# Loading half of the last piece of w_out earlier, swapping the engines that cast its rows, and moving one x step, in a fused attention and GELU kernel

## The chip, the cores and the metric

The kernel runs on one core of a Trainium2 chip. The metric is the device time of one execution in microseconds (us). A profiled execution also has a span, which is some 1.8 us shorter than its time.

## The reference

```python
def _attn_ref(q, k, v):              # 8 batches, 8 heads, 576 rows, 64 columns
    q_s = softmax(q, axis=-1)        # over the 64 columns   (written out in the original)
    k_s = softmax(k, axis=2)         # over the 576 rows
    kv = np.einsum('bhsd,bhse->bhde', k_s, v)
    return np.einsum('bhsd,bhde->bhse', q_s, kv)

x = attn_out.transpose(0, 2, 1, 3).reshape(4608, 512)
h = x @ w_in                         # 512 -> 2048
g = 0.5 * h * (1.0 + erf(h / sqrt(2)))
out = g @ w_out                      # 2048 -> 512
```

## The kernel before

A batch goes through these steps, and the words are used below as the program uses them. **exp_q, exp_k** (ScalarE), **norm_q** (VectorE and GpSimd: sums and a multiplication), **transposes** of q (TensorE) and their evacuation (the copy out of the memory that TensorE writes to) to qT, **kv** (TensorE, from exp(k) and the cast v), **x** = q times kv (TensorE), its evacuation to xT (ScalarE and VectorE), **h** = x times w_in (TensorE), **gelu** (ScalarE), **y** = g times w_out (TensorE), **y_out** (evacuation of y).

The y of batch 0 runs while batch 1's front is computed. Its w_out arrives in four pieces of four rows, where a row t is a set of 128 of its rows; a row t is cast to bf16 before the y matmuls of t. The change touches how the last piece (rows 12 to 15) comes in, and the order at the end of that stretch. All loads below are in one queue.

```python
    load_main(1, "q", q, 2)
    load_pair(1, "k", k, 2)             # batch 1's k in two halves
    wo.append(load_wo(3))               # rows 12 and 13 of w_out
    for hp in range(2):
        load_v1(hp)
    load_wo_row(wo[3], 2)               # row 14
    load_wo_row(wo[3], 3)               # row 15
    load_v1(2)
    load_v1(3)
    # ... cut ...
    exp_q(1, parts=2)
    exp_k(1, parts=2)
    table(AF.Gelu)
    cast_wo(2, wo[2])                   # rows 8 to 11, VectorE
    # ... cut: PSUM tiles ...
    norm_q(1, 0, 2)
    norm_q(1, 1, 2, nc.vector)
    cast_wo(3, wo[3], 0, 1)             # row 12, VectorE
    cast_wo(3, wo[3], 1, 1)             # row 13, VectorE
    for hp in range(HP):
        cast_v(1, hp, nc.gpsimd)
    # ... cut ...
    for t in range(12):
        y_part(t, range(J))             # four y matmuls a row
    load(3)
    cast_wo(3, wo[3], 2, 1, "s")        # row 14, ScalarE
    cast_wo(3, wo[3], 3, 1, "s")        # row 15, ScalarE
    y_part(12, range(J))
    y_part(13, range(J))
    tp_quarters(1, tps)                 # transposes
    kv_mm(1, 0)
    tp_quarters_evac(1, tps, 0, "v")
    tp_quarters_evac(1, tps, 1, "s")
    kv_norm(1, 0)
    y_part(14, range(J))
    y_part(15, (0, 1))
    # ... cut: tiles of x ...
    x_mm(1, 0)
    kv_mm(1, 1)
    y_out(0, yps[0], 0)
    x_evac(1, 0, "s")
    x_evac(1, 1)
    kv_norm(1, 1)
    y_out(0, yps[1], 1, "s")
    y_part(15, (2, 3))
    # then the h matmuls of batch 1
```

The softmax here doesn't subtract the row's maximum and nothing guards it: scores larger than these inputs give would overflow.

Of the kernel before, what the change touches and what calls it, by code (L numbers as in the profile page):

```python
# [8 lines left out]
FP32 = mybir.dt.float32  # L9
# [7 lines left out]
def kernel(  # L17
# [16 lines left out]
    nc = tc.nc  # L34
    B, H, S, D = q.shape
# [5 lines left out]
    HP = H // 2  # L41
    NDM = DM // 128
    NDF = DF // 128
    NS = S // 64
# [3 lines left out]
    f32in = ctx.enter_context(tc.tile_pool(name="f32in", bufs=2))  # L48
# [29 lines left out]
    def table(func):  # L78
        nc.scalar.activation(out=scr[:, 1:2], in_=scr[:, 0:1], func=func)  # L79

    st = [dict() for _ in range(B + 1)]

    def load_main(b, name, t, parts=1):
        f = f32in.tile([128, 2048], FP32, tag=name + "f")
        f = f.rearrange("p (h f) -> p h f", h=H)
        st[b][name + "f"] = f
        src = t[b, :, 0:M, :].rearrange("h (p j) d -> p h (j d)", j=J)
        n = H // parts
        for i in range(parts):
            nc.sync.dma_start(out=f[:, i * n:(i + 1) * n, :], in_=src[:, i * n:(i + 1) * n, :])  # L90

    def load_pair(b, name, t, parts=1):
        f = f32in.tile([128, HP, NS * D], FP32, tag=name + "f")
        st[b][name + "f"] = f
        src = t[b].rearrange("h (p n) d -> (h p) (n d)", n=NS).rearrange("(x q) f -> q x f", q=128)
        n = HP // parts
        for i in range(parts):
            h0 = i * n
            if b == 0 and name == "k" and i == 0:

                nc.scalar.dma_start(out=f[:, 0, :], in_=src[:, 0, :])
                h0 = 1
            nc.sync.dma_start(out=f[:, h0:(i + 1) * n, :], in_=src[:, h0:(i + 1) * n, :])

    def load_v1(i):

        if i == 0:
            st[1]["vf"] = f32in.tile([128, HP, NS * D], FP32, tag="vf", name="f")
        src = v[1].rearrange("h (p n) d -> (h p) (n d)", n=NS)
        nc.sync.dma_start(out=st[1]["vf"][:, i, :], in_=src[i * 128:(i + 1) * 128, :])  # L110

    def load(b):
        load_main(b, "q", q)
        load_pair(b, "k", k)
        load_pair(b, "v", v)
# [11 lines left out]
    def exp_q(b, parts=1):  # L127

        e = attn_sb.tile([128, J, H, D], BF16, tag="eq")
        st[b]["eq"] = e  # L130
        dst = e.rearrange("p j h d -> p h j d")
        src = st[b]["qf"]
        if b == B:
            src = src.rearrange("p j h d -> p h j d")
        else:
            src = src.rearrange("p h (j d) -> p h j d", j=J)
        if parts == 1:
            sets = [(slice(i, None, 4), slice(u, None, 4)) for i, u in ((0, 0), (1, 1), (2, 3), (3, 2))]
        else:
            sets = []  # L140
            for h in (0, 4):
                sets += [(slice(h + i, h + i + n), slice(h + u, h + u + n))
                         for i, u, n in ((0, 0, 2), (2, 3, 1), (3, 2, 1))]
        for i, u in sets:
            nc.scalar.activation(out=dst[:, i], in_=src[:, u], func=AF.Exp)  # L145

    def exp_k(b, parts=1):
        n = HP // parts
        for i in range(0, HP, n):
            nc.scalar.activation(  # L150
                out=ek[b % 2][:, i:i + n],
                in_=st[b]["kf"][:, i:i + n].rearrange("p x (n d) -> p x n d", n=NS),
                func=AF.Exp,
            )
# [33 lines left out]
    def kv_mm(b, half):  # L188


        if "kv" not in st[b]:
            kv_tiles(b)
        for n in range(NS):
            for i in range(2):
                for hh in range(2):
                    hp = 2 * half + i
                    pr = slice(hh * 64, hh * 64 + 64)
                    c = slice((hh ^ i) * 64, (hh ^ i) * 64 + 64)
                    nc.tensor.matmul(  # L199
                        st[b]["kv"][hp][c, 0:D + 1], ek[b % 2][pr, hp, n, :],  # L200
                        v_aug[b % 2][pr, hp, n, 0:D + 1], start=(n == 0), stop=(n == NS - 1),
                    )
# [25 lines left out]
    def norm_q(b, i=0, n=1, eng=None):  # L228

        eng = eng or nc.gpsimd  # L230
        eq = st[b]["eq"]
        w = H // n
        hs = slice(i * w, (i + 1) * w)
        qsum = small.tile([128, J, w], FP32, tag="qsum")
        recq = small.tile([128, J, w], FP32, tag="recq")
        nc.vector.reduce_sum(out=qsum, in_=eq[:, :, hs, :], axis=AX.X)  # L236
        nc.vector.reciprocal(recq, qsum)  # L237
        eng.tensor_tensor(  # L238
            out=eq[:, :, hs, :], in0=eq[:, :, hs, :],
            in1=recq.unsqueeze(3).to_broadcast([128, J, w, D]), op=ALU.mult,  # L240
        )
# [51 lines left out]
    def x_tile(b, hp, pool, tag):  # L293
        if "xT" not in st[b]:
            st[b]["xT"] = attn_sb.tile([128, HP, M], BF16, tag="xT", name="xT")
        st[b][f"x{hp}"] = pool.tile([128, M], FP32, tag=tag, name="ps")
# [32 lines left out]
    def x_evac(b, hp, eng="v"):  # L329
        ps = st[b][f"x{hp}"]  # L330
        if eng == "v":
            nc.vector.tensor_copy(out=st[b]["xT"][:, hp, :], in_=ps)  # L332
        else:
            nc.scalar.copy(out=st[b]["xT"][:, hp, :], in_=ps)  # L334
# [33 lines left out]
    def y_mm(c, ps, j, t):  # L368
        nc.tensor.matmul(  # L369
            ps, st[c]["g"][:, t, j * 128:(j + 1) * 128], wo_bf[:, t, :],  # L370
            start=(t == 0), stop=(t == NDF - 1),
        )

    def y_out(c, ps, j, eng="v"):
        y_sb = moe_sb.tile([128, DM], FP32, tag="y_sb")
        if eng == "v":
            nc.vector.tensor_copy(out=y_sb, in_=ps)  # L377
        else:
            nc.scalar.copy(out=y_sb, in_=ps)
        if c < B:  # L380
            dst = out[c * S:c * S + M, :].rearrange("(p j) n -> p j n", j=J)[:, j, :]
            nc.sync.dma_start(out=dst, in_=y_sb)
        else:
            for b2 in range(2):
                r0 = (2 * j + b2) * S + M
                nc.sync.dma_start(out=out[r0:r0 + R, :], in_=y_sb[b2 * R:(b2 + 1) * R, :])
# [69 lines left out]
    def load_wo(i):  # L456
        w = wst.tile([128, 4, DM], FP32, tag="w")
        src = moe_w_out[i * 512:(i + 1) * 512, :]
        if i == 0:
            for h in range(2):  # L460
                nc.sync.dma_start(
                    out=w[:, 2 * h:2 * h + 2],
                    in_=src[256 * h:256 * h + 256].rearrange("(p c) f -> p c f", c=2),
                )
            return w
        src = src.rearrange("(p c) f -> p c f", c=4)
        if i == 3:
            nc.sync.dma_start(out=w[:, 0:2], in_=src[:, 0:2])
            return w
        nc.sync.dma_start(out=w, in_=src)  # L470
        return w
# [5 lines left out]
    def cast_wo(i, w, c0=0, n=4, eng="v"):  # L477
        o, w = wo_bf[:, 4 * i + c0:4 * i + c0 + n, :], w[:, c0:c0 + n]
        if eng == "v":
            nc.vector.tensor_copy(out=o, in_=w)  # L480
        else:
            nc.scalar.copy(out=o, in_=w)
# [17 lines left out]
    wi = [load_wi(i) for i in range(5)]  # L500
    wo = [load_wo(i) for i in range(3)]
    load_main(1, "q", q, 2)
    load_pair(1, "k", k, 2)
    wo.append(load_wo(3))
    for hp in range(2):
        load_v1(hp)
    load_wo_row(wo[3], 2)
    load_wo_row(wo[3], 3)
    load_v1(2)
    load_v1(3)  # L510
    load(2)
    nc.vector.memset(zeros32, 0.0)  # L512
# [5 lines left out]
    table(AF.Exp)  # L518
    exp_q(0, parts=2)
    exp_k(0, parts=2)  # L520
    norm_q(0, 0, 2)
    norm_q(0, 1, 2, nc.vector)
# [48 lines left out]


    exp_q(1, parts=2)
    exp_k(1, parts=2)
    table(AF.Gelu)
    cast_wo(2, wo[2])
    tps = [pool.tile([128, HP, J, 64], BF16, tag=tag, name="tp")
           for pool, tag in ((psum_a, "a"), (psum_h, "h"))]
    yps = [psum_h.tile([128, DM], FP32, tag="h", name="ps") for j in range(2)]
    yps += [psum_y.tile([128, DM], FP32, tag="y", name="ps") for j in range(2)]  # L580
    norm_q(1, 0, 2)
    norm_q(1, 1, 2, nc.vector)
    cast_wo(3, wo[3], 0, 1)
    cast_wo(3, wo[3], 1, 1)
    for hp in range(HP):
        cast_v(1, hp, nc.gpsimd)

    def y_part(t, js):
        for j in js:
            y_mm(0, yps[j], j, t)  # L590
# [1 line left out]
    for t in range(12):  # L592
        y_part(t, range(J))
    load(3)
    cast_wo(3, wo[3], 2, 1, "s")
    cast_wo(3, wo[3], 3, 1, "s")
    y_part(12, range(J))
    y_part(13, range(J))
    tp_quarters(1, tps)
# [2 lines left out]
    tp_quarters_evac(1, tps, 1, "s")  # L602
    kv_norm(1, 0)
    y_part(14, range(J))
    y_part(15, (0, 1))
    x_tile(1, 0, psum_a, "a")
    x_tile(1, 1, psum_h, "h")
    x_mm(1, 0)
    kv_mm(1, 1)
    y_out(0, yps[0], 0)  # L610
    x_evac(1, 0, "s")
    x_evac(1, 1)
    kv_norm(1, 1)
    y_out(0, yps[1], 1, "s")
    y_part(15, (2, 3))



# [19 lines left out]

    exp_q(2, parts=2)
    exp_k(2)  # L640
    exp_k(3)
    exp_q(3)
# [73 lines left out]
```

## Time and profile before

| | before |
|---|---|
| time, median of the first 3 runs | 279.8 us (279.75 to 280.11) |
| span of the profiled run | 277.7 us |
| TensorE busy | 269.1 us, 97% of the span |
| first y matmul of batch 0 | 27.76 us |
| y matmul of row 12, due at 38.12 | 38.59 us |
| first h matmul of batch 1 | 43.92 us |

The last three rows are starts read from the timeline of TensorE. "Due" is the start that an unbroken stream would have had; the prediction works it out. A group in a timeline has its start, its length, the engine, the line, what is written and read, and the number of instructions; a bracket at the end names an idle time before the group and who ended it.

### The profile page before, as it was taken

How to read it: one execution, taken by the hardware profiler on the slowest of the kernel's cores; microseconds unless marked ns; L12 is line 12 of the kernel's file. 1: busy time of each engine (PE TensorE's matmuls, PEld its weight loads, DVE VectorE, ACT ScalarE, POOL GpSimd, SP SyncE). 2: the span in 40 equal slices, each digit the busy share in tenths (PEclk: the TensorE clock that was granted, in tenths of full speed). 3: DMA queues.
4: the chain of work that ended last, by engine and by line, in shares of the span. 5: the costliest groups of instructions: out<-in, count | busy, mean ns of one | idle time of the engine just before them, and what ended most of it. 6: DMA issues, size and time to landing. Idle time of an engine off the chain costs nothing.

```text
span 277.7 us, 4630 instructions
## 1 busy us (share of the span) xinstructions
PE 269.1 (97%) x1938; PEld 126.0 (45%) x1966; DVE 100.6 (36%) x154; ACT 158.9 (57%) x247; POOL 32.5 (12%) x26
## 2 busy tenths in 40 slices
PE   7899999999999999999999999999999999999995
PEld 3444444444444444444444444444444444444443
DVE  2876565319752540173008400751015200130012
ACT  4867586789377716791669246943683363126400
POOL 1510051002020220013000500050005000000000
PEclk9999999999999999999999999999999999999999
DMA  7999999964992149612980199117402500210033
GB/s 258 399 393 431 397 400 404 402 249 108 296 334 62 73 106 269 273 40 89 278 315 38 47 220 389 61 46 192 110 0 78 151 0 0 78 76 0 2 76 77
DMA packets 44980, 50.10 MB, mean 180 GB/s; under 512 B 20384, under 2 KB 29856, under 8 KB 44704
## 3 DMA queue, kind: packets, MB, share of 16 engines
q1 hardware_dynamic: 44560, 49.39, 52.8%
q10 hardware_dynamic: 400, 0.43, 0.5%
q8 instruction: 15, 0.25, 0.3%
q14 instruction: 5, 0.04, 0.1%
HBM read 36.70 MB, written 9.44 MB: 166 GB/s over the span
## 4 chain that ended last, share of the span: by engine, by line
PE 84%; DMA 11%; DVE 2%; issue 1%; ACT 0%; SPq 0%
PE ps L369 40%; PE ps L341 40%; DMA f<-in_q_dram 6%; DMA w<-in_moe_w_in_dram 3%; DMA f<-in_v_dram 2%; PE kv L199 2%; PE ps L308 1%; PE ps L394 1%; DVE qsum L236 1%; DVE e L238 1%; ACT e L145 0%; PE ps L313 0%; PE tp L272 0%; DVE recq L237 0%; DVE wo_bf L480 0%
## 5 line engine op out<-in xcount | busy, mean ns | idle before, releaser
L341 PE MATMUL ps<-xT,wi_bf 128*128 128x512 bf16 x557 | 124.1, 379 | 0.6
L369 PE MATMUL ps<-wo_bf,g 128*128 128x512 bf16 x543 | 122.1, 379 | 1.9 <-issue 1.1
L347 ACT ACTIVATE g<-ps 128x512 bf16<-128x512 f32 x142 | 83.5, 598 | 66.9 <-PE ps L341 66.8
L341 PEld LDWEIGHTS <-wi_bf 128*128 128x128 bf16 x576 | 56.4, 98 | 67.9 <-issue 0.5
L369 PEld LDWEIGHTS <-g 128*128 128x128 bf16 x560 | 54.0, 98 | 65.0 <-issue 1.0
L377 DVE COPY y_sb<-ps 128x512 f32<-128x512 f32 x33 | 22.7, 687 | 82.6 <-PE ps L369 79.5
L238 POOL TENSOR_TENSOR e<-e,recq 128x2048 bf16<-128x2048 bf16 (+1 forms) x9 | 25.7, 2855 | 176.6 <-DVE recq L237 148.5
L162 DVE CAST v_aug<-f 128x576 bf16<-128x576 f32 x24 | 16.4, 745 | 46.6 <-DMA f<-in_v_dram 46.6
L236 DVE TENSOR_REDUCE qsum<-e 128x16 f32<-128x1024 bf16 (+1 forms) x13 | 21.1, 1621 | 14.0 <-ACT e L145 14.0
L334 ACT CAST xT<-ps 128x512 bf16<-128x512 f32 x18 | 9.9, 588 | 26.8 <-PE ps L308 16.8
L145 ACT ACTIVATE e<-f 128x512 bf16<-128x512 f32 (+1 forms) x42 | 20.5, 556 | 3.7 <-DMA f<-in_q_dram 3.6
L150 ACT ACTIVATE ek<-f 128x2304 bf16<-128x2304 f32 (+1 forms) x10 | 17.2, 1728 | 0.5 <-DMA f<-in_k_dram 0.4
L332 DVE CAST xT<-ps 128x512 bf16<-128x512 f32 x17 | 11.0, 686 | 17.0 <-PE ps L308 14.1
L79 ACT ACT_TABLE_LOAD x9 | 11.5, 1283 | 2.8 <-issue 2.7
L487 PE MATMUL ps<-zeros 128*128 128x512 f32 x14 | 8.5, 772 | 1.5 <-DVE zeros L512 1.5
L145 ACT ACT_TABLE_LOAD x7 | 9.0, 1283 | 0.1
L446 DVE CAST wi_bf<-w 128x512 bf16<-128x512 f32 x12 | 7.1, 621 | 2.3 <-DMA w<-in_moe_w_in_dram 1.9
L199 PEld LDWEIGHTS <-ek 64*64 64x64 bf16 x576 | 6.4, 105 | 2.1 <-issue 0.5
L199 PE MATMUL kv<-v_aug,ek 64*64 64x65 bf16 x576 | 6.8, 193 | 0.4 <-POOL v_aug L162 0.4
L238 DVE TENSOR_TENSOR e<-e,recq 128x1024 bf16<-128x1024 bf16 x4 | 6.3, 1574 | 0.1
L487 PEld LDWEIGHTS ps<-zeros 128*128 128x128 f32 x14 | 3.4, 252 | 5.7 <-issue 4.3
L308 PE MATMUL ps<-qT,kvc 64*64 64x512 bf16 x62 | 5.6, 390 | 0.3 <-DVE kvc L218 0.2
(40 smaller groups left out, 49.5 us busy)
## 6 DMA issues: line engine op xcount, KB each, us to landing
out_dram<-y_sb SPq DMA_DIRECT2D x32, 256.0 KB, 2.4
f<-in_k_dram SPq DMA_DIRECT2D x6, 1152.0 KB, 9.8
f<-in_v_dram SPq DMA_DIRECT2D x6, 1152.0 KB, 11.6
f<-in_q_dram SPq DMA_DIRECT2D x6, 1024.0 KB, 7.7
w<-in_moe_w_in_dram SPq DMA_DIRECT2D x6, 512.0 KB, 9.0
f<-in_v_dram SPq DMA_DIRECT2D x8, 288.0 KB, 6.3
f<-in_q_dram SPq DMA_DIRECT2D x4, 512.0 KB, 8.8
w<-in_moe_w_out_dram SPq DMA_DIRECT2D x2, 1024.0 KB, 11.8
```

Source lines behind the costliest of these rows:

```text
L79: nc.scalar.activation(out=scr[:, 1:2], in_=scr[:, 0:1], func=func)
L145: nc.scalar.activation(out=dst[:, i], in_=src[:, u], func=AF.Exp)
L150: nc.scalar.activation(out=ek[b % 2][:, i:i + n], in_=st[b]["kf"][:, i:i + n].rearrange("p x (n d) -> p x n d", n=NS), func=AF.Exp,)
L162: eng.tensor_copy(out=o, in_=i)
L199: nc.tensor.matmul(st[b]["kv"][hp][c, 0:D + 1], ek[b % 2][pr, hp, n, :], v_aug[b % 2][pr, hp, n, 0:D + 1], start=(n == 0), stop=(n == NS - 1),
L236: nc.vector.reduce_sum(out=qsum, in_=eq[:, :, hs, :], axis=AX.X)
L238: eng.tensor_tensor(out=eq[:, :, hs, :], in0=eq[:, :, hs, :], in1=recq.unsqueeze(3).to_broadcast([128, J, w, D]), op=ALU.mult,)
L341: nc.tensor.matmul(ps, wi_bf[:, dm, t * 128:(t + 1) * 128], st[c]["xT"][:, dm, :], start=(dm == 0), stop=(dm == NDM - 1),)
L347: nc.scalar.activation(out=st[c]["g"][:, t, :], in_=ps, func=AF.Gelu)
L369: nc.tensor.matmul(ps, st[c]["g"][:, t, j * 128:(j + 1) * 128], wo_bf[:, t, :], start=(t == 0), stop=(t == NDF - 1),)
L377: nc.vector.tensor_copy(out=y_sb, in_=ps)
L487: nc.tensor.matmul(ps, z[:, 0:128], z, start=True, stop=True)
```

## The change

The intent is to take the hole at row 12 out of TensorE's stream. The first half of the last w_out piece goes ahead of the second half of batch 1's k; ScalarE casts rows 12 and 13 between the two halves of exp(k), and VectorE takes rows 14 and 15. Since the stream then runs earlier, the first x is put one y matmul later, so that the kv step behind it does not meet a v that is still being cast, and two y_outs go ahead of x.

```diff
@@ loads @@
     load_main(1, "q", q, 2)
-    load_pair(1, "k", k, 2)
+    load_k1(0)
     wo.append(load_wo(3))
+    load_k1(1)
@@ batch 1's front @@
     exp_q(1, parts=2)
-    exp_k(1, parts=2)
+    exp_k(1, parts=2, part=0)
+    cast_wo(3, wo[3], 0, 1, "s")
+    cast_wo(3, wo[3], 1, 1, "s")
+    exp_k(1, parts=2, part=1)
     table(AF.Gelu)
...
     norm_q(1, 1, 2, nc.vector)
-    cast_wo(3, wo[3], 0, 1)
-    cast_wo(3, wo[3], 1, 1)
...
-    cast_wo(3, wo[3], 2, 1, "s")
-    cast_wo(3, wo[3], 3, 1, "s")
+    cast_wo(3, wo[3], 2, 1)
+    cast_wo(3, wo[3], 3, 1)
@@ end of batch 0's y @@
     y_part(14, range(J))
-    y_part(15, (0, 1))
+    y_part(15, (0, 1, 2))
+    y_out(0, yps[0], 0)
+    y_out(0, yps[1], 1, "s")
     # tiles of x
     x_mm(1, 0)
     kv_mm(1, 1)
-    y_out(0, yps[0], 0)
     x_evac(1, 0, "s")
     x_evac(1, 1)
     kv_norm(1, 1)
-    y_out(0, yps[1], 1, "s")
-    y_part(15, (2, 3))
+    y_part(15, (3,))
```

(`load_k1` loads one half of batch 1's k; `exp_k` gets an argument for one half.)

More of the change, by code (lines that the diff above doesn't have):

```diff
@@ L103, in load_pair, with load_k1 @@
             nc.sync.dma_start(out=f[:, h0:(i + 1) * n, :], in_=src[:, h0:(i + 1) * n, :])
+    def load_k1(i):
+        if i == 0:
+            st[1]["kf"] = f32in.tile([128, HP, NS * D], FP32, tag="kf", name="f")
+        src = k[1].rearrange("h (p n) d -> (h p) (n d)", n=NS).rearrange("(x q) f -> q x f", q=128)
+        nc.sync.dma_start(out=st[1]["kf"][:, 2 * i:2 * i + 2, :], in_=src[:, 2 * i:2 * i + 2, :])
     def load_v1(i):
@@ L145, in exp_q, with exp_k @@
             nc.scalar.activation(out=dst[:, i], in_=src[:, u], func=AF.Exp)
-    def exp_k(b, parts=1):
+    def exp_k(b, parts=1, part=None):
         n = HP // parts
-        for i in range(0, HP, n):
+        for i in range(0, HP, n) if part is None else (part * n,):
             nc.scalar.activation(
```

## The prediction

> **What bounds the kernel now.** I read the page's busy line and its chain that ended last first, then the list of waits, then the timeline of the stretch that the change touches (36 to 46 us), engine by engine.
>
> ```profile
> PE 269.1 (97%) x1938; PEld 126.0 (45%) x1966; DVE 100.6 (36%) x154; ACT 158.9 (57%) x247; POOL 32.5 (12%) x26
> ...
> PE 84%; DMA 11%; DVE 2%; issue 1%; ACT 0%; SPq 0%
> ```
>
> TensorE has work in 97% of the span, and 84% of the chain that ended last is TensorE; the rest is the front (loads and batch 1's softmax) that a step of TensorE once waited for. So a change can only pay by closing a hole in TensorE's stream. The chain shows one such hole after the start, at the row of w_out that the change is about:
>
> ```profile
> 33.56 1.23 DVE qsum L236
> 34.79 0.02 issue
> 34.82 0.25 DVE recq L237
> 35.07 1.12 DVE qsum L236
> 36.19 0.02 issue
> 36.22 0.26 DVE recq L237
> 36.48 0.02 issue
> 36.50 1.70 DVE e L238
> 38.20 0.35 DVE wo_bf L480
> 38.55 0.04 issue
> 38.59 1.89 PE ps L369 x8
> ```
>
> The columns are start, duration and what (us). VectorE normalises batch 1's q until 38.20, only then casts row 12 of w_out, and the y matmuls of that row start at 38.59. The timeline of TensorE around it:
>
> ```profile
> 27.76 10.52 PE L369 MATMUL ps<-wo_bf,g 128*128 128x512 bf16 x47
> 38.59 1.89 PE L369 MATMUL ps<-wo_bf,g 128*128 128x512 bf16 x8 [0.30 <-DVE wo_bf L480]
> 40.40 0.71 PE L272 MATMUL tp<-identity,e 64*64 64x64 bf16 x64
> 40.93 0.54 PE L199 MATMUL kv<-v_aug,ek 64*64 64x65 bf16 x36
> 41.40 1.47 PE L369 MATMUL ps<-wo_bf,g 128*128 128x512 bf16 x5
> 42.80 0.41 PE L308 MATMUL ps<-qT,kvc 64*64 64x512 bf16 x4
> 43.04 0.51 PE L199 MATMUL kv<-v_aug,ek 64*64 64x65 bf16 x36
> 43.48 0.60 PE L369 MATMUL ps<-wo_bf,g 128*128 128x512 bf16 x2
> ```
>
> The printed wait is 0.30, counted from the end of a matmul that is still draining. The loss is larger. Twelve rows times four matmuls at one every 0.216 us from 27.76 put the next start at 27.76 + 48 x 0.2159 = 38.12; it came at 38.59. **The hole costs 0.47 us.** Nothing else there is a wait: the steps from transposes to kv, to y, to x leave 0.09 to 0.14 us each, as the same steps do in later batches where all operands are old (there they are the 0.05 and 0.16 us "issue" pieces). From 46 us on, the list of waits has no TensorE wait of note, so what TensorE gains or loses before 46 us should be carried to the end unchanged.
>
> **What the Trainium skill says.** (1) "TensorE: Matmul & The Clock Gate", section "Wait — 56ns, not 53.3ns?": warm matmuls of 512 columns start 215.7 ns apart. The trace agrees: 22 y matmuls in 4.91 us, the last one 0.38 long, make (4.91 - 0.38) / 21 = 0.216 us. (2) "DMA: Bandwidth & Descriptors", section "Queues, rings and completion order": each DMA engine takes descriptors in ring order. Here batch 1's two k halves and the first half of the last w_out piece were issued in that order and landed in it, about 35.1, 36.5 and 37.75; so issuing the w_out half before the second k half should swap the two landings. (3) "ScalarE: Activation LUTs", section "What ACT_TABLE_LOAD costs": 1283 ns for the load and about 1380 ns of drain for a switch of set. The trace has the 1.28 us, but the next activation begins right behind (37.72 + 1.28, then 39.01), so I charge 1.28 alone. (4) "Perfetto Trace Analysis", section "Optimizing Scalar/DVE Operations", says that breaking up instructions may let work complete sooner where these engines are not saturated but cause bubbles elsewhere. That is the case; the row casts were already split, and the change moves two of them to the engine that is free earlier.
>
> **The change part by part.** Nothing is added or removed but one split of an existing pair of issues: same bytes, same four row casts, same matmuls; two casts trade VectorE for ScalarE and the other two the reverse.
>
> Rows 12 and 13. The landing views and ScalarE's timeline give the times:
>
> ```profile
> DMA to landing us min/median/max: 9.0/9.0/9.0
> ...
> 35.11 1.16 ACT L150 ACTIVATE ek<-f 128x1152 bf16<-128x1152 f32 x1 [0.19 <-DMA f<-in_k_dram]
> 36.54 1.16 ACT L150 ACTIVATE ek<-f 128x1152 bf16<-128x1152 f32 x1 [0.26 <-DMA f<-in_k_dram]
> 37.72 1.28 ACT L79 ACT_TABLE_LOAD   x1
> 39.90 1.25 ACT L482 CAST wo_bf<-w 128x512 bf16<-128x512 f32 x2 [0.69 <-DMA w<-in_moe_w_out_dram]
> ...
> 41.30 1.37 POOL L162 CAST v_aug<-f 128x576 bf16<-128x576 f32 x2 [1.30 <-DMA f<-in_v_dram]
> ```
>
> The w_out half was issued at 28.75 and landed 9.0 later, 37.75. Put ahead of the second k half it lands 512 KB after the first: the stretches view gives 404 GB/s between 12 and 50 us, so 1.30 us after about 35.1, at 36.4. ScalarE has finished the first half of exp(k) at 35.11 + 1.16 = 36.27, so it casts from 36.4: row 12 at 36.4 + 0.62 = 37.0, row 13 at 37.65 (0.62 a row, from the 1.25 for two). TensorE wants row 12 at 38.12 and row 13 at 38.98. Both are over a microsecond early. **Gain: the whole 0.47 us**, at that place.
>
> Second half of exp(k). It lands at 37.75 instead of 36.5, runs to 38.9, the table load goes to 40.2, its dummy activation to 40.4. ScalarE then evacuates the transposes, which TensorE, now 0.47 earlier (39.93 to 40.46), hands over at about 40.7 (before: 0.8 after their start). No wait on the path.
>
> Rows 14 and 15 on VectorE. Row 14 lands at 39.90 and takes 0.41 there (the two casts before took 0.41 each), 40.31; TensorE wants it after the first kv half, at 41.40 - 0.47 = 40.93. Row 15 lands about 256 KB later, 40.5, cast by 40.95, wanted at 41.8. The VectorE evacuation of transposes then starts at 40.95 rather than 40.7, ends 41.65, kv norm 42.1.
>
> First x one group later. x now follows seven y matmuls: 40.93 + 7 x 0.216 + 0.1 = 42.54, against 42.80. Its operands are there at 42.1. kv of the second half follows at 42.78; its last v cast on GpSimd ends at 41.30 + 1.37 = 42.67. Just free: in the old order x would start at 42.33 and kv would have waited, which is what this part of the change is for.
>
> What it costs. Behind that kv half only one y matmul is left in place of two, so the h matmuls that need x follow sooner. Before, x at 42.80 was followed by ScalarE's evacuation from 43.25 to 43.84 and the h matmul at 43.92, with no gap. Now: x 42.54, evacuation 42.99 to 43.58 (0.45 after x and 0.59 long, as before; y_out of yps[1] on ScalarE is ahead of it, from about 42.46 to 43.05, just about fitting), so x is usable at 43.65. TensorE is through with kv and the one y matmul at 42.54 + 0.68 + 0.23 = 43.45. **New wait: about 0.20 us.** The second x half, its kv norm and the two remaining y_outs end well before they are wanted.
>
> Sum: -0.47 + 0.20 = -0.27 us; 279.8 - 0.27 = 279.5.
>
> **The rivals.** (a) The hole goes and no wait replaces it: -0.47, 279.3. For it: the 0.20 rests on delays of 0.45 and 0.07 us taken from single instructions. Against: the y matmul was the only cover. (b) The wait is moved, not removed: if landings come in order but later, or if ScalarE's later exp(k) and table load push the evacuation of transposes beyond 41.0, x waits for it, and with GpSimd's v casts, which are tied to the landings and not to TensorE, nothing of the gain is left: 279.8. GpSimd's slack is only about 0.1 us, so this is the serious one. (c) The reorder disturbs the queue, for example the blocked issue at 23.5 us (5.1 us long for one k half) now holds others up, and batch 1's front slips by some tenths: 280.1. Against it: the DMA share is full throughout and bytes are unchanged. (d) Front jitter: the hole hangs on the q load that ends near 32.3; in executions where it lands later the hole is wider than 0.47, and the change, whose rows have 1.1 us of slack, gains more: down to 279.2.
>
> **Range and chances.** The largest part possible is half a microsecond in 280, or 0.2%; the three runs before spread over 0.36 us. No rival reaches 2% (5.6 us) in either direction. I take 279.5, with (a) and (d) at the low end and (b) and some of (c) at the high one: 279.1 to 279.9. Faster by over 2%: 0.005; within 2%: 0.99; slower: 0.005.
>
> **What would show it.** Right: no TensorE wait on wo_bf near 38.1; the y stream of 27.8 us runs on for 56 matmuls, transposes near 39.9; ScalarE casts two rows between the halves of exp(k) near 36.4; x near 42.5; a wait of TensorE on xT of 0.1 to 0.3 us near 43.5; the gelu stream from 46 us on some 0.27 us earlier, and the end too. Step wrong: row casts on ScalarE after 38 (the landing did not move), a wait of the second kv half on v_aug (rival b), an x that waits for qT. The total would be wrong if any load that is first used after 46 us arrived later, or if the front (q's first half, 32.3 us) moved.

## The result, and the profile after

The changed kernel took 279.31 us in the median of 6 runs (279.26 to 279.55); the kernel before, with three more runs, 279.73 (279.33 to 280.11). The ratio is 0.9988, with a 95% interval of 0.9975 to 1.0001. Ratios are the mean time of one kernel's fast runs over that of the other's of the same rounds, so not quite the ratio of the medians.

From the page of the changed kernel, the busy line and the chain that ended last:

```profile
PE 270.9 (98%) x1966; PEld 125.6 (45%) x1966; DVE 100.8 (36%) x154; ACT 158.9 (57%) x247; POOL 32.5 (12%) x26
...
PE 94%; DMA 4%; POOL 0%; DVE 0%; issue 0%; SPq 0%
```

The busy sums of TensorE are not to be compared: the first trace has 1938 of its matmul records, this one 1966. The chain can be: 94% of it is TensorE now, and the 11% that went through loads in the kernel before is 4%, because no step in the middle of the stream waits for batch 1's softmax any more. Now the timeline of TensorE in the changed kernel, the same stretch as in the prediction:

```profile
27.79 12.25 PE L376 MATMUL ps<-wo_bf,g 128*128 128x512 bf16 x56
39.97 0.71 PE L279 MATMUL tp<-identity,e 64*64 64x64 bf16 x64
40.50 0.54 PE L206 MATMUL kv<-v_aug,ek 64*64 64x65 bf16 x36
40.97 1.68 PE L376 MATMUL ps<-wo_bf,g 128*128 128x512 bf16 x7
42.58 0.41 PE L315 MATMUL ps<-qT,kvc 64*64 64x512 bf16 x4
42.82 0.51 PE L206 MATMUL kv<-v_aug,ek 64*64 64x65 bf16 x36
43.26 0.39 PE L376 MATMUL ps<-wo_bf,g 128*128 128x512 bf16 x1
43.67 1.02 PE L348 MATMUL ps<-xT,wi_bf 128*128 128x512 bf16 x4
```

All 56 y matmuls run in one piece: the hole is gone. The x step starts at 42.58 where it started at 42.80. And the last y matmul, at 43.26, is followed by the first h matmul 0.41 us later; two matmuls of 512 columns start 0.216 to 0.23 apart, so this is a new gap of 0.18 us. It carries no bracket because the modelled end of the y matmul hides it. ScalarE in the same trace shows both the new casts and the cause of the gap:

```profile
34.91 1.16 ACT L157 ACTIVATE ek<-f 128x1152 bf16<-128x1152 f32 x1 [0.19 <-DMA f<-in_k_dram]
36.13 1.14 ACT L489 CAST wo_bf<-w 128x512 bf16<-128x512 f32 x2
37.56 1.16 ACT L157 ACTIVATE ek<-f 128x1152 bf16<-128x1152 f32 x1 [0.29 <-DMA f<-in_k_dram]
...
42.47 0.59 ACT L386 COPY y_sb<-ps 128x512 f32<-128x512 f32 x1 [0.69 <-PE ps L376]
43.04 0.59 ACT L341 CAST xT<-ps 128x512 bf16<-128x512 f32 x1
```

Rows 12 and 13 are cast right behind the first half of exp(k), 1.4 us or more before TensorE wants them. The evacuation of x ends at 43.04 + 0.59 = 43.63, and the h matmul that reads it starts at 43.67.

The first h matmul of batch 1 comes at 43.67 against 43.92, 0.25 us earlier, and the shift stays: the second kv step of later batches starts at 64.71 against 64.97 and the one of batch 7 at 184.71 against 184.97. From the first h matmul of batch 1 to the last matmul of the kernel the two traces have 230.19 and 230.20 us.

This gives a measure that is far finer than the times. **Start of h** is the start of the first h matmul of batch 1 less that of the first y matmul, both read from the timeline: 43.92 - 27.76 = 16.16 before, 43.67 - 27.79 = 15.88 after. In all fourteen traces what follows it takes 230.19 to 230.20 us, so a difference in it is a difference in the time, apart from where the stream begins. That start is not fixed either: the first y matmul comes at 27.76 to 28.32 us in these traces, and this enters the time in full.

### The profile page after: what moved, and what is told of

Same layout as the page of the kernel before. It is cut to its first block, busy times and chain, and to the rows that moved or that the text cites. A ratio compares the mean times of both kernels' runs of the same rounds, so it can differ in the third digit from the quotient of the medians.

```text
span 277.5 us, 4658 instructions
## 1 busy us (share of the span) xinstructions
PE 270.9 (98%) x1966; PEld 125.6 (45%) x1966; DVE 100.8 (36%) x154; ACT 158.9 (57%) x247; POOL 32.5 (12%) x26
## 4 chain that ended last, share of the span: by engine, by line
PE 94%; DMA 4%; POOL 0%; DVE 0%; issue 0%; SPq 0%
PE ps L348 44%; PE ps L376 44%; DMA f<-in_v_dram 2%; PE kv L206 2%; PE ps L315 2%; DMA f<-in_q_dram 2%; PE ps L401 1%; PE pair L348 1%; POOL v_aug L169 0%; PE ps L320 0%; PE tp L279 0%; SPq L103 0%; DVE kvc L225 0%; DVE y_sb L406 0%; DVE rec L224 0%
## 5 line engine op out<-in xcount | busy, mean ns | idle before, releaser
L376 PE MATMUL ps<-wo_bf,g 128*128 128x512 bf16 x560 | 124.1, 379 | 0.0
L487 DVE CAST wo_bf<-w 128x2048 bf16<-128x2048 f32 (+1 forms) x5 | 4.5, 907 | 6.1 <-DMA w<-in_moe_w_out_dram 6.1
```

The costliest lines, as they stand in the source:

```text
L376: nc.tensor.matmul(ps, st[c]["g"][:, t, j * 128:(j + 1) * 128], wo_bf[:, t, :], start=(t == 0), stop=(t == NDF - 1),)
```

## The experiments

Three quantities of each trace are used: the start of h as above; the **hole** before row 12, that is the start of the transposes less that of the first y matmul less the 12.18 us of an unbroken stream; and the **phase** p, the start of the first half of batch 1's exp(k) on ScalarE (which waits for its load) less that of the first y matmul. The phase tells how late the loads of q and k are against TensorE; it changes when the loads land earlier or later, and also when TensorE's y stream itself begins earlier or later. All three are worked out from the starts before rounding.

| trace | p | hole | start of h |
|---|---|---|---|
| before | 7.35 | 0.47 | 16.16 |
| before again | 7.33 | 0.45 | 16.14 |
| x later only | 7.00 | 0.11 | 15.99 |
| load order only | 6.92 | 0.04 | 15.73 |
| before, delayed | 7.76 | 1.04 | 16.74 |
| change | 7.12 | 0 | 15.88 |
| change again | 6.88 | 0 | 15.88 |
| change, delayed | 8.13 | 0 | 16.37 |
| y_out behind | 7.55 | 0 | 15.88 |
| no cover | 7.07 | 0 | 16.10 |
| casts, old loads | 7.05 | 0.02 | 15.90 |
| casts only | 7.45 | 0 | 16.07 |
| kv pair by pair | 6.83 | 0 | 15.83 |
| split cast | 6.82 | 0 | 15.70 |

**The change again.** No edit.

> The changed kernel unaltered, with five rounds, to narrow the ratio (0.9988 so far, its interval reaching 1.0001). My theory, from the two traces (hole of 0.47 us gone, a new wait of about 0.18 us on xT, all later starts 0.25 us earlier up to the last matmul): ratio 0.9991, 0.25 us faster. Rival (front jitter: executions of the kernel before in which batch 1's q lands later lose more than 0.47): ratio 0.9985 to 0.9988, and a spread of the kernel before of 0.5 us or more against about 0.3 for this one. In its trace: y stream of 56 matmuls without a break, first h matmul of batch 1 about 0.41 us after the last y matmul before it instead of 0.22.

It took 279.42 us (279.34 to 279.67), the kernel before in the same rounds 279.68 (279.26 to 279.84): ratio 0.9996 (0.9983 to 1.0008). So the gain is in neither call clear of zero, and it was smaller here. The trace has the same start of h to the hundredth, 15.88, with the loads 0.24 us earlier against TensorE (p 6.88 instead of 7.12): within this range the changed kernel does not depend on them. The kernel before spread more in these rounds too, 0.58 against 0.33 us, but over nine runs against five (more on this below).

**Casts only, x in its old place.**

```diff
-    y_part(15, (0, 1, 2))
-    y_out(0, yps[0], 0)
-    y_out(0, yps[1], 1, "s")
+    y_part(15, (0, 1))
     ...  (the tail of the kernel before)
```

> The new load order and row casts, but x and its y_outs in their old place (x after six y matmuls, two y matmuls left behind kv). My theory: x starts near 42.37, the second kv half begins near 42.6 but must wait for GpSimd's last v cast (ends about 42.77) at its first use of the fourth pair, so it ends about where it ends in the changed kernel; the two y matmuls behind it then cover x's evacuation, no wait on xT; first h matmul at about 43.70, within 0.05 us of the changed kernel's 43.67. So moving x is worth nothing: 0.22 to 0.25 us faster than before, equal to the change. Rival (the move is needed: the wait on v_aug comes on top): first h matmul at 43.9 or later, gain 0.05 us or less.

It took 279.33 us (279.19 to 279.54), ratio 0.9989 (0.9976 to 1.0003), which can't be told from the change. In its trace the wait on v is there as forecast:

```profile
42.42 0.41 PE L315 MATMUL ps<-qT,kvc 64*64 64x512 bf16 x4
42.66 0.20 PE L206 MATMUL kv<-v_aug,ek 64*64 64x65 bf16 x2
43.07 0.47 PE L206 MATMUL kv<-v_aug,ek 64*64 64x65 bf16 x34 [0.21 <-POOL v_aug L169]
```

Two kv matmuls run, then the third stops for the last v cast. The loads of this execution came late (p 7.45), so the stop was 0.39 us (from the due start 42.67 to 43.07) and the start of h 16.07, not the 15.85 or so that I had expected. So my theory that moving x is worth nothing failed in this trace, and the rival's number was met: the first h matmul came at 43.92, as in the first trace of the kernel before. The times, 0.9989 here against 0.9996 for the change in the same rounds, do not show that loss. What follows from the trace is that the move of x trades this wait, which varies with the loads, for the fixed one on xT.

**x later only.** The kernel before with the tail of the change.

```diff
-    y_part(15, (0, 1))
+    y_part(15, (0, 1, 2))
+    y_out(0, yps[0], 0)
+    y_out(0, yps[1], 1, "s")
     ...  (the tail of the change)
```

> The kernel before with only x one matmul group later and its y_outs ahead. My theory: the hole of 0.47 us at the row of w_out stays, the new wait on xT of about 0.2 us comes on top: 0.2 us slower than before (ratio 1.0007), first h matmul near 44.1 against 43.92. Rival (the move is harmless by itself and the missing gain is elsewhere): equal to before, no wait at the first h matmul.

Ratio 1.001 (0.9998 to 1.0023), median 279.76 us: slower by about what was expected, though the interval touches one. The trace is clear: start of h 15.99 = 15.69 + 0.11 of hole + 0.19 of the new gap. The surprise is the hole of 0.11, where the same code in the first trace of before had 0.47. Everything up to row 12 is equal in the two programs; what differs is that the loads stood 0.35 us earlier against TensorE (exp(k) began 0.13 us earlier, and the y stream 0.22 us later). This changed my theory: **the hole is not a constant of the program.** With VectorE's chain from the landing of q to the cast of row 12 being fixed in length, the hole should be p - 6.88, and zero below.

**kv pair by pair.** The casts-only kernel; in the second kv half of batch 1 the loop over pairs of heads is outermost, so that the last v is wanted later.

```diff
-        for n in range(NS):
-            for i in range(2):
+        order = [(n, i) for n in range(NS) for i in range(2)]
+        if (b, half) == (1, 1):
+            order = [(n, i) for i in range(2) for n in range(NS)]
+        for n, i in order:
```

> As the casts-only kernel, but the second kv half of batch 1 does all nine steps of its first pair of heads before those of its second pair, so that the last v cast on GpSimd is wanted some 0.2 us later. My theory: neither the wait on v_aug nor the one on xT is left; x near 42.37, first h matmul near 43.50, 0.17 us earlier than in the changed kernel, and 0.4 us faster than before (ratio 0.9985). Rival ([...]the kv half takes up to twice its 0.41 us): first h matmul at 43.7 or later and no gain over the change.

Start of h 15.83: no wait on v nor on xT, but the kv half, which is followed by y 0.44 us after its start otherwise, took 0.58 (42.79 to 43.37). So 0.05 us was gained over the change instead of 0.17, and the rival's size was largely right. The absence of the wait on v is no merit of the new order, though: in this execution the last v cast ended at 42.54, before the kv half began at 42.79, so that the old order would not have waited either. Ratio 0.9995 (0.9983 to 1.0008).

**Before again, and the useless load.** The next three runs test the dependence on the loads. The first has no edit. The other two are the kernel before and the change with 256 KB more in the queue ahead of batch 1's q:

```diff
+    nc.sync.dma_start(out=zeros32, in_=moe_w_out[0:128, :])
     load_main(1, "q", q, 2)
```

(The tile's memset and the warm-up are moved ahead of the loads in the program text; their order on the engines is unchanged.)

> The kernel before, unaltered: the noise of a ratio of equals, and a further trace of the hole. The traces so far say that the hole is set by how late batch 1's loads land against TensorE's stream: take p, the start of the first half of exp(k) of batch 1 less the start of the first y matmul. With p = 7.35 (first trace of before) the hole was 0.47, with p = 7.00 (x later only, same front) 0.12. My theory now: hole = p - 6.88, zero below, so here anything from 0 to 0.6 us, and that formula within 0.05. Rival: the hole is a fixed 0.47 us of the program, whatever p. Ratio 1.0000 with an interval of about 0.0012 to either side.

> The kernel before with one useless load of 256 KB put into the queue ahead of batch 1's q (into the tile of zeros that the warm-up matmuls have done with), so that all of batch 1's loads land about 0.65 us later against TensorE. My theory: p becomes 7.5 to 8.1, the hole p - 6.88, so 0.6 to 1.2 us, and the time 0.4 to 0.65 us longer than before (ratio 1.0015 to 1.0023). Rival (front not bound by these landings): no change.

> The changed kernel with the same useless load. My theory: rows 12 and 13 still come in time, so no hole at the row of w_out, but the last v cast gates the second kv half: excess over a stream without waits is the larger of 0.19 and p - 7.2, so 0.3 to 0.9 us; the change stays ahead of the delayed kernel before by about 0.3 us and by no more, since the next load of the same queue gates behind the one that was moved. Rival (the change takes the stream off the landings altogether): excess stays near 0.19, the time equals that of the undelayed change, and the lead over the delayed kernel before grows to 0.6 us or more.

Before again: ratio 0.9998 (0.9986 to 1.001), so two equal kernels differ by up to that interval; its hole is 0.45 with p 7.33, as p - 6.88 says, but a hole fixed at 0.47 would look the same there; what speaks against that rival is the delayed run and the two small holes. Its five runs spread over 0.18 us only, while eleven runs of the same kernel in the same rounds spread over 0.78. Before, delayed: 280.13 us, ratio 1.0031 (1.0018 to 1.0044), above the forecast of 1.0015 to 1.0023, though the interval reaches into it; in the traces its start of h is 0.58 us later than in the first of before. The hole shows in its timeline:

```profile
27.81 10.52 PE L369 MATMUL ps<-wo_bf,g 128*128 128x512 bf16 x48
39.21 1.89 PE L369 MATMUL ps<-wo_bf,g 128*128 128x512 bf16 x8 [0.88 <-DVE wo_bf L480]
```

Due at 27.81 + 10.36 = 38.17, the row came at 39.21: 1.04. The formula gives 0.88 for p 7.76, so it is 0.16 off here. Some 0.06 of it is that the two halves of q's exponentials ran without the pause that the other four traces with a hole on VectorE's path show, and p is measured behind them. The rest is VectorE's chain: from its first qsum to the cast of row 12 it took 4.65 us (34.08 to 38.73) against 4.56 (33.56 to 38.12), so the chain is not quite fixed in length. Change, delayed: 279.88 us, ratio 1.0013 (1.0001 to 1.0025). Its stream still has all 56 y matmuls in one piece, and waits further on:

```profile
40.54 0.78 PE L206 MATMUL kv<-v_aug,ek 64*64 64x65 bf16 x36
...
43.15 0.20 PE L206 MATMUL kv<-v_aug,ek 64*64 64x65 bf16 x2
43.57 0.47 PE L206 MATMUL kv<-v_aug,ek 64*64 64x65 bf16 x34 [0.23 <-POOL v_aug L169]
43.98 0.39 PE L376 MATMUL ps<-wo_bf,g 128*128 128x512 bf16 x1
44.20 1.03 PE L348 MATMUL ps<-xT,wi_bf 128*128 128x512 bf16 x4
```

The second kv half stops for the last v, and behind it y and h follow without the gap, since xT is ready by then. The first kv half stops too: after two matmuls it waits for the second v cast, which ends at 40.78, and y follows 0.71 us after its start instead of 0.47. Together with 0.05 before x these two stops, 0.24 and 0.39, make the 0.68 us by which the start of h exceeds 15.69. The expected p - 7.2 would be 0.93: p does not fix when the last v is cast, which ended 7.56 us after the start of exp(k) here and 7.86 us after it in the trace of the change. So the change does not take the stream off the loads: it moves the place where they bind from row 12 to the casts of v. The lead over the delayed kernel before is 0.0018 of the time, 0.5 us, between the 0.3 that I expected and the 0.6 of the rival; in the two traces it is 16.74 - 16.37 = 0.37, though the loads stood 0.37 us later in the second. The start of h of the delayed change is 0.49 us later than that of the undelayed one, so the rival's claim that it would not notice the delay falls.

**Split cast.** The casts-only kernel with the last v cast shared by GpSimd and ScalarE.

```diff
-    for hp in range(HP):
+    for hp in range(HP - 1):
         cast_v(1, hp, nc.gpsimd)
+    cast_v_part(1, 3, 0, 5, nc.gpsimd)
...
     tp_quarters_evac(1, tps, 1, "s")
+    cast_v_part(1, 3, 5, 9, nc.scalar)
```

> The casts-only kernel (x in its old place) with the last v cast of batch 1 split: its first five of nine steps on GpSimd, the other four on ScalarE, which is idle there. My theory: the last operand of the second kv half is ready some 0.3 us earlier, so neither v_aug nor xT is waited for unless p is above 7.3; first h matmul 15.69 to 15.75 us after the first y matmul, against 15.88 in both traces of the change, and about 0.19 us faster than the change in the mean (ratio to before about 0.9983 to 0.999). Rival (the wait on v_aug is one for the landing, not for the cast): first h matmul at 15.85 or later.

Start of h 15.70, the stream without any wait (15.69), and 0.18 us less than the change:

```profile
42.77 0.51 PE L214 MATMUL kv<-v_aug,ek 64*64 64x65 bf16 x36
43.21 0.61 PE L384 MATMUL ps<-wo_bf,g 128*128 128x512 bf16 x2
43.65 1.03 PE L356 MATMUL ps<-xT,wi_bf 128*128 128x512 bf16 x4
```

The times can't show it: 279.31 us, ratio 0.9996 (0.9984 to 1.0008). Its q and k were early in this execution (p 6.82), but its last v was not: the two parts of that cast began 14.25 and 14.28 us after the first y matmul, and in the change's own trace the last v cast began at 14.31. A whole cast on GpSimd takes 0.69 us there and would have ended at some 14.97, where the third kv matmul is due at 14.82. So by my estimate the split took away a wait of 0.15 to 0.2 us; a run of the casts-only kernel in the same phase, which would show it, was not made. I do not claim that it beats the change.

**Load order only, and casts with the old loads.** One half of the first part of the change each:

```diff
 (load order only, on the kernel before)
-    load_pair(1, "k", k, 2)
+    load_k1(0)
     wo.append(load_wo(3))
+    load_k1(1)

 (casts with the old loads, on the change)
     load_k1(0)
-    wo.append(load_wo(3))
     load_k1(1)
+    wo.append(load_wo(3))
```

> The kernel before with only the load order of the change: the w_out half ahead of the second k half, all casts where they were (rows 12 and 13 on VectorE behind the normalisation of q). A look at the trace. My theory: row 12 waits for VectorE's normalisation, not for its landing, so the hole is the same function of p as before, p - 6.88 (about 0 to 0.5 us), with the cast starting right behind the normalisation. Rival (the landing alone was late): no hole, the cast before 37 us.

> The changed kernel with the old load order: k whole, then the w_out half; casts on ScalarE between the halves of exp(k) as in the change. A look at the trace. My theory: the rows land about 2.64 us after the first k half, so the casts start then, row 12 is ready at p + 3.3 after the first y matmul and wanted at 10.36: hole p - 7.04, that is 0 to 0.4 us, only 0.16 less than before; both halves of the change are needed. Rival (the engine alone does it): no hole whatever p.

With the load order alone the second half of exp(k) starts at 37.60 instead of 36.5, so the two landings were swapped and row 12 was there before that; but VectorE casts it where it did, behind the normalisation:

```profile
36.34 1.68 DVE L245 TENSOR_TENSOR e<-e,recq 128x1024 bf16<-128x1024 bf16 x1
37.95 0.75 DVE L487 CAST wo_bf<-w 128x512 bf16<-128x512 f32 x2
```

The hole was 0.04 with p 6.92, exactly p - 6.88. With the casts alone ScalarE idles 1.49 us for the landing and casts at 37.87, 2.66 us behind the start of exp(k); the hole was 0.02 with p 7.05, as p - 7.04 says. The second does not separate its two theories well, since at this p mine asked for almost no hole; that the casts now hang on the landing is shown, that they would be late at a larger p is only argued.

**No cover, and y_out behind.** Two tests of the gap before the first h matmul.

```diff
 (no cover, on the change)
-    y_part(15, (0, 1, 2))
+    y_part(15, (0, 1, 2, 3))
...
-    y_part(15, (3,))

 (y_out behind, on the change)
-    y_out(0, yps[1], 1, "s")
...
     x_evac(1, 0, "s")
+    y_out(0, yps[1], 1, "s")
```

> The changed kernel with all four y matmuls of the last row ahead of x, so that none is left behind the second kv half. A look at the trace. My theory: the h matmul waits for x's evacuation, 1.09 us after x's start, whatever lies between: x at about 15.01 after the first y matmul, first h matmul at 16.10, behind a wait of about 0.40 us instead of 0.18. Rival (what is waited for is not xT but something that does not move with x, the banks of the y results or the queue of y_outs): first h matmul stays within 0.05 of 15.88.

> The changed kernel with ScalarE's y_out of the second y result behind its evacuation of x instead of ahead of it. A look at the trace. My theory: that y_out just fits ahead of x's evacuation, so the evacuation starts at the same time after x (0.45 us) and the first h matmul stays at 15.88, the wait at 0.18; the h matmuls of the second bank, which needs that y_out, may then wait some 0.05 us. Rival (the y_out put ahead of the evacuation makes the wait): evacuation 0.1 us or more earlier and first h matmul at 15.75 or earlier.

Without cover the start of h is 16.10, as forecast, and the gap is now large enough to carry its cause:

```profile
43.06 0.41 PE L315 MATMUL ps<-qT,kvc 64*64 64x512 bf16 x4
43.30 0.51 PE L206 MATMUL kv<-v_aug,ek 64*64 64x65 bf16 x36
44.15 0.81 PE L348 MATMUL ps<-xT,wi_bf 128*128 128x512 bf16 x3 [0.34 <-ACT xT L341]
```

The h matmul comes 1.09 us after x, as it does in the change (43.67 - 42.58), with one y matmul in between or with none. With the y_out behind, the evacuation started 0.45 us after x as before and the start of h stayed at 15.88. So the gap is the evacuation of x alone, and not the y_out that was put ahead of it. This trace shows one thing more. Its loads came late (p 7.55, the last v cast ended 15.12 us after the first y matmul), and its second kv half took 0.55 us instead of 0.44; yet the h matmul came 1.09 us after x all the same, so a short wait for v hides behind the one on xT. In the casts-only trace, where the last v cast ended at 15.17 and x stood in its old place, the start of h was 16.07. That difference of 0.19 is what the move of x is worth when v is this late.

## Why the prediction was right or wrong

The time forecast was 279.5 with a range of 279.1 to 279.9; it came out at 279.31, and the ratio of 0.9988 (0.33 us) has 0.27 inside its interval, as has the later 0.9996. Both intervals hold zero too, so the times do not confirm the forecast; the traces carry the argument.

- **"The hole costs 0.47 us"**: right for that trace, shown by the unbroken stream of the changed kernel. Wrong as a property of the kernel: other executions with the same code up to row 12 had 0.45, 0.11 and 0.04.
- **Rows 12 and 13**: cast from 36.13, forecast 36.4; the forecast start of the second half of exp(k) was 37.75 against 37.56. Both differences are about those of the front of this execution (its exp(k) began 0.20 earlier). Right, and the load order only run shows that VectorE's queue, not the landing, had made row 12 late.
- **"First x one group later"**: x at 42.58 against 42.54, right. The reason given, that kv would have waited in the old place, is shown by the casts-only run. In the change's own trace the last cast ended just before it was wanted.
- **"New wait: about 0.20 us"**: 0.18, and the no-cover run shows its cause, 1.09 us from x to h, where the prediction put together 1.11 from 0.45, 0.59 and the way to TensorE.
- **"-0.27 us"**: the starts of h differ by 0.28 in these two traces, and the shift is carried to the end unchanged, as said. That the one trace before which the sum was built on had a large hole is luck: with a hole of 0.04 or 0.11 the same change would have come out as a small loss.
- **The rivals.** (a) did not happen: the gap is there. (b), a wait for v that eats the gain, was rightly called the serious one: it takes 0.11 us, still hidden, at p 7.55 (y_out behind), and is open in the delayed change. (c) did not show: the blocked issue of about 5.1 us only passed from the second k half to the w_out half. (d) was the right idea, but it named one side only: it reckoned with executions whose loads are later than in the first trace, while that trace was among the late ones. Of the eleven other traces without the useless load two have a larger p (7.45 and 7.55) and nine a smaller one. They are of different programs, and the kernel before itself was traced only twice, with 7.35 and 7.33. But p differs between two executions of one program (the change, 7.12 and 6.88), and between the four traces of one chip and one set of rounds (6.83 to 7.45), so neither the program nor the chip alone sets it.

The step that was mis-sized is therefore the first, the hole. The stream without waits has a start of h of 15.69 (16.16 - 0.47, 16.14 - 0.45 and 15.73 - 0.04 agree). The kernel before adds the hole, 0.04 to 0.47 in the undelayed traces; the change adds a fixed 0.19. So, at equal phase and in the undelayed traces, **the change gains up to 0.28 us where the loads are late and loses up to 0.15 us where they are early**: the load order only trace, which still had the casts and the tail of before, is 15.73 and thus ahead of the change's 15.88. No timed run shows such a loss. The two ratios, 0.33 and 0.11 us with intervals of about 0.35 to either side, agree with this without testing it. The kernel before spread more than the change in both sets of rounds, but that is no evidence either: in the third set the same kernel spread over 0.18 us in one row of runs and 0.78 in the other. How much of the spread is the phase and how much the start of the y stream, which differs by 0.56 us between traces, stays open, since timed executions have no trace.

## What to carry to other kernels

Where an engine waits for a chain that begins with a load, one trace gives one draw of the wait; look at a second trace, or delay the load on purpose, before taking its length for the gain. Taking the first wait out only helps up to the next consumer of the same queue, so list what else lands there and when it is wanted. And a stream of matmuls can only be moved forward as far as there is other work to cover the evacuations in it: here one y matmul less of cover cost 0.19 of the 0.47 us.

## What the Trainium skill lacked or had wrong

- "TensorE: Matmul & The Clock Gate", section "Back-to-back issue gap", gives some 131 ns a matmul at 512 columns for a stream of weight loads and matmuls and says that 216 ns over-counts. In these traces 216 ns is the spacing of just such a stream (22 y matmuls, each with its weight load, in 4.91 us, the last one 0.38 long: 4.53 / 21 = 0.216), and the section "Wait — 56ns, not 53.3ns?" is the one that holds.
- "ScalarE: Activation LUTs", section "What ACT_TABLE_LOAD costs", adds about 1.38 us of drain to the load. Here the activation before the load ends at 38.72, the load runs from 38.74 to 40.02, and the next activation starts at 40.04.
- "TensorEngine Tiling (Array Packing)" says that a change of tiling mode drains the engine, but no time. Here a step from 128x128 to 64x64 matmuls left 0.09 us beyond the usual spacing, and in the step back the first y matmul started about 0.14 us after the last kv matmul.
- No page says how much the landing of queued loads moves against the compute from one execution to the next. Undelayed traces here lie between p 6.82 and 7.55, and between p 6.92 and 7.35 the wait before row 12 was 0.04 to 0.47 us.
